# Fused memory attention and expert layer: the opening's loads, softmax and small tables in another order

## The chip, the cores and the metric

The kernel runs on one core of a Trainium2 chip. A core has five engines with queues of their own: TensorE (PE, and PEld for its weight loads), VectorE (DVE), ScalarE (ACT), GpSimd (POOL) and SyncE (SP, which issues most DMAs). The metric is device microseconds of one execution; lower is better.

## The reference

Eight batches, eight heads, 576 tokens, head size 64 and 32 memory slots. The attention output is the input of a gate that picks one of eight experts for each token.

```python
a = softmax(phi, axis=2)                    # phi: (8, 8, 576, 32), over the tokens
k_m = einsum('bhsm,bhsd->bhmd', a, k)       # 32 memory keys of each head
v_m = einsum('bhsm,bhsd->bhmd', a, v)
attn = softmax(q @ k_m.T / 8, axis=-1)      # (8, 8, 576, 32)
x = (attn @ v_m) as (4608, 512)             # heads side by side
logits = x @ w_gate + modality_bias[modality_id]
e = argmax(logits); gate_w = softmax(logits)[e]
out = gate_w * (relu(x @ w1[e]) @ w2[e])    # w1: (8, 512, 1024), w2: (8, 1024, 512)
```

## The kernel before

For each batch the kernel first builds the memory: the maximum of `phi` over the tokens (`first_max`, `mem_top`), exponentials (`mem_exp`), their sums (`mem_sums`), and products with `k` and `v` (`first_products`). The divided keys are turned by TensorE into `kT` and the values into `kvT` (`first_divide`, `first_odd`, `first_keys`, `first_values`). Scores (`first_scores`), a softmax over 32 slots (`soften`, `first_weights`) and a split in two parts of reduced precision (`first_split`: `xah` high, `xal` low) follow. The values are multiplied into the expert's first weights (`value_products`: `vwh` high, `vwl` low), so that the hidden layer (`hidden`, line 831) is a product of `xa` with `vw`, and the output (`outputs`, line 868) a product of `hh`/`hl` with `w2h`/`w2l`. `raw` is the expert's weights as loaded. All products of the expert stage are made three times (high by high, low by high, high by low).

The expert of the first token is guessed from the modality alone (`first_bias` on GpSimd, `preferred` and `guess` on VectorE), and its `w1` and `w2` are loaded by SP as soon as the guess is known. `mid` (the modality of all tokens) and `wg` (the gate's weights) are two small tables; `spread_row` spreads a row of the modality bias over all partitions by a product with ones, and ScalarE copies it to `known`.

Part 0 of batch 0 (256 of 576 tokens) is the opening. It is worked on in two groups of heads, `g` 0 and 1. The order of all instructions is made when the kernel is built: `plan_first` lists the steps of the opening in one order, `TAKES` gives each step's assumed time on each engine, and `weave` puts them between the experts' steps. Each engine then runs its own list strictly in that order. While TensorE would have nothing to do in the opening, `warm_small` and `warm` give it products of zeros that nobody reads, called fillers here (lines 168 and 161; `BUSY` says how many). TensorE's output banks are handed out from pools: `pair_of_banks(0)` is one buffer, so that a step that takes it waits until the reader of the step before is done.

## Time and profile before

| | |
|---|---|
| median of 3 runs | 379.02 us (378.89 to 379.66) |
| the profiled execution's own time | 379.99 us |
| its span, first to last instruction | 378.2 us |
| TensorE busy in the span | 370.8 us (98%) |
| VectorE, ScalarE, GpSimd busy | 248.5, 139.5, 45.9 us |
| granted clock of TensorE, mean | 0.995 |

The time is the span and 1.8 us around it. The granted clock has two levels in the profile's rows: 1.00 is 2.4 GHz, 0.50 is 1.2 GHz. Fillers count as busy, so the busy share does not tell how much of the opening is work.

### The profile page before, as it was taken

The page shows a single profiled execution, that of the slowest core. Times are in us where ns is not written, and L with a number is a line of the kernel's source. Part 1 is how long each engine was busy: PE and PEld are TensorE (multiplying, and loading weights), DVE is VectorE, ACT ScalarE, POOL GpSimd, SP SyncE. Part 2 cuts the span into 40 slices and gives each one's busy share as a digit, 9 for nine tenths or more (in the row PEclk, how much of TensorE's full clock was granted, in tenths as well). Part 3 has the DMA queues.
Part 4 walks back from the last instruction along what each step waited for, and adds up shares of the span by engine and source line. Part 5 has one row for each costly group of instructions (what it writes and reads, how often), then busy time and mean ns, then how long its engine had stood idle before and what let it go on. Part 6 is the DMA issues. An engine that isn't in the chain of part 4 may idle for free.

```text
span 378.2 us, 9988 instructions
## 1 busy us (share of the span) xinstructions
PE 370.8 (98%) x4045; PEld 309.8 (82%) x4045; DVE 248.5 (66%) x618; ACT 139.5 (37%) x328; POOL 45.9 (12%) x110
## 2 busy tenths in 40 slices
PE   7999999999999999999999999999999999999996
PEld 2767887889869897898987889797987979697986
DVE  4688767885958797868855689657874448750400
ACT  2283333534335055323414244431623306240401
POOL 3138030013130030004000030004000000000000
PEclk9899999999999999999999999999999999999999
DMA  8998769968958747583654637760232102321112
GB/s 289 348 378 233 111 98 279 285 116 269 316 107 257 259 73 137 170 301 61 111 166 131 239 69 133 204 212 2 56 99 86 29 2 55 119 63 30 31 34 56
DMA packets 93979, 56.89 MB, mean 150 GB/s; under 512 B 69732, under 2 KB 75108, under 8 KB 93924
## 3 DMA queue, kind: packets, MB, share of 16 engines
q1 hardware_dynamic: 93648, 55.87, 54.3%
q8 instruction: 33, 0.54, 0.6%
q10 hardware_dynamic: 276, 0.30, 0.2%
q14 instruction: 22, 0.18, 0.2%
HBM read 37.28 MB, written 18.87 MB: 148 GB/s over the span
## 4 chain that ended last, share of the span: by engine, by line
PE 92%; DVE 4%; DMA 1%; ACT 1%; issue 1%; ACTq 0%; POOL 0%; POOLq 0%; DVEq 0%
PE pe L868 49%; PE pe L831 27%; PE pair L408 4%; PE pe L776 2%; PE pair L571 2%; PE pe L912 2%; PE pair L713 1%; DMA row<-n_moe_modality_bias_dram 1%; PE pair L776 1%; PE pair L433 1%; PE pair L150 1%; PE pair L593 1%; PE pe L433 1%; DVE mx L628 0%; DVE a L624 0%
## 5 line engine op out<-in xcount | busy, mean ns | idle before, releaser
L868 PE MATMUL pe<-w2h,hh 128*128 128x512 f32 x280 | 111.2, 397 | 0.0
L868 PE MATMUL pe<-w2h,hl 128*128 128x512 f32 x280 | 109.3, 390 | 0.0
L868 PE MATMUL pe<-w2l,hh 128*128 128x512 f32 x280 | 107.1, 390 | 0.0
L848 DVE SCALAR_TENSOR_TENSOR hl<-pe,hh 128x256 fp32r<-128x256 f32 (+2 forms) x158 | 56.9, 390 | 37.5 <-ACT hh L844 36.7
L844 ACT ACTIVATE hh<-pe 128x256 fp32r<-128x256 f32 (+2 forms) x158 | 52.7, 362 | 32.9 <-PE pe L831 32.2
L868 PEld LDWEIGHTS pe<-w2h,hh 128*128 128x128 f32 x280 | 52.6, 188 | 12.0 <-DVE vwl L798 0.8
L868 PEld LDWEIGHTS pe<-w2l,hh 128*128 128x128 f32 x280 | 52.5, 188 | 11.2
L868 PEld LDWEIGHTS pe<-w2h,hl 128*128 128x128 f32 x280 | 52.6, 188 | 9.8
L881 ACT ACTIVATE ob<-pe,gates 128x512 f32<-128x512 f32 x35 | 23.9, 689 | 76.6 <-PE pe L868 38.9
L831 PE MATMUL pe<-xbh,vwh 128*128 128x320 f32 x128 | 40.2, 314 | 0.1
L831 PE MATMUL pe<-xbh,vwl 128*128 128x320 f32 x128 | 39.5, 309 | 0.0
L831 PE MATMUL pe<-xbl,vwh 128*128 128x320 f32 x128 | 39.5, 309 | 0.0
L831 PE MATMUL pe<-xah,vwh 128*128 128x256 f32 x124 | 35.2, 287 | 0.5 <-ACT xah L679 0.5
L831 PE MATMUL pe<-xah,vwl 128*128 128x256 f32 x124 | 34.9, 283 | 0.0
L831 PE MATMUL pe<-xal,vwh 128*128 128x256 f32 x124 | 34.9, 283 | 0.0
L831 PEld LDWEIGHTS pe<-xah,vwh 128*128 128x128 f32 x124 | 23.6, 191 | 2.8 <-ACT xah L679 1.6
L831 PEld LDWEIGHTS pe<-xbh,vwh 128*128 128x128 f32 x128 | 24.0, 188 | 1.4 <-issue 0.5
L344 POOL COPY ts<-tm 32x4 f32<-32x4 f32 x24 | 5.0, 210 | 164.4 <-DVE tm L336 163.6
L831 PEld LDWEIGHTS pe<-xbl,vwh 128*128 128x128 f32 x128 | 24.0, 188 | 0.3
L831 PEld LDWEIGHTS pe<-xbh,vwl 128*128 128x128 f32 x128 | 24.0, 188 | 0.0
L831 PEld LDWEIGHTS pe<-xal,vwh 128*128 128x128 f32 x124 | 23.7, 192 | 0.2
L831 PEld LDWEIGHTS pe<-xah,vwl 128*128 128x128 f32 x124 | 23.7, 192 | 0.0
(174 smaller groups left out, 466.7 us busy)
## 6 DMA issues: line engine op xcount, KB each, us to landing
out_dram<-ob SPq DMA_DIRECT2D x72, 128.0 KB, 2.4
q_sb<-in_q_dram SPq DMA_DIRECT2D x112, 72.0 KB, 3.1
kv_sb<-in_k_dram SPq DMA_DIRECT2D x6, 1152.0 KB, 6.3
kv_sb<-in_v_dram SPq DMA_DIRECT2D x6, 1152.0 KB, 9.7
ph<-in_phi_dram SPq DMA_DIRECT2D x13, 288.0 KB, 8.2
kv_sb<-in_k_dram SPq DMA_DIRECT2D x4, 576.0 KB, 6.0
kv_sb<-in_v_dram SPq DMA_DIRECT2D x4, 576.0 KB, 7.1
raw<-in_moe_w_dram SPq DMA_DIRECT2D x2, 1024.0 KB, 7.7
```

What stands on the lines that cost most here:

```text
L150: nc.tensor.transpose(dst, src, ident[:rows, :rows])
L344: nc.gpsimd.tensor_copy(ts_[BL * a:BL * (a + 1)], live["tm"][BL * o:BL * (o + 1)])
L408: nc.tensor.matmul(live["kvp"][M * j:M * (j + 1), g], lhsT=pe[half, j, c * M:(c + 1) * M], rhs=kv_sb[half, :, j, c * D:(c + 1) * D], start ...
L433: nc.tensor.matmul(to[g][M * j:M * (j + 2), 0:2 * D].rearrange("p (j d) -> p j d", j=2), lhsT=pe[half, c, j:j + 2].rearrange("p j m -> p ( ...
L571: nc.tensor.matmul(sc[g][M * j:M * (j + 1), a, 0:QC * BL], lhsT=kvT[b][rows, 0, M * j:M * (j + 1)], rhs=qT[rows, j, a], start=True, stop=T ...
L776: nc.tensor.matmul(pvs[g][M * j:M * (j + 1), :], lhsT=vT[b][rows, j, :], rhs=raw1[rows, j, cols], start=True, stop=not more, tile_position ...
L831: nc.tensor.matmul(ph[:, 0:n], lhsT=(vl if k == 2 else vh)[:, g, cols], rhs=xl if k == 1 else xh, start=(g == k == 0), stop=(g == NG - 1 a ...
L844: nc.scalar.activation(hs[0][:, f, h0:h0 + p1 - p0], live["ph", f][:, p0:p1], AF.Relu)
L848: nc.vector.scalar_tensor_tensor(hl, live["ph", f][:, p0:p1], 0.0, hh.bitcast(F32), op0=ALU.max, op1=ALU.subtract)
L868: nc.tensor.matmul(po, lhsT=tile_columns(hl if n == 1 else hh, f, t), rhs=(w2l if n == 2 else w2h)[:, f, :], start=(f == n == 0), stop=(f ...
L881: nc.scalar.activation(ob, po, AF.Copy, scale=gate_of(b, t))
L912: nc.tensor.matmul(po, lhsT=x, rhs=w2s[w][:, f, cols], start=(f == i == 0), stop=(f == FCH - 1 and i == 2),)
```

## The change

All of it is in the steps up to some 30 us. The halves of the first `phi` go out one behind the other on SP's queue, where one half went out on ScalarE's queue; the two tiny loads of ScalarE (`mid0` and the bias row) then come first there. `mid` and `wg`, which SP issued between the halves of `w1`, come behind the expert's weights and the rest of the queries. `preferred` stands ahead of the maximum's end. There is one small filler less ahead, and three more of 256 columns behind the exponentials' broadcast; `spread_row` moves from there behind the products with `v`. The first scores are made in two halves, each behind its own turn of the queries. In the softmax, group 1's subtraction and group 0's `xal` go to GpSimd. The first hidden products (`ha`) stand ahead of the value products of the second half of `w1`. `prepare` and `biases` (the modality tables, on GpSimd) come last.

```diff
-    BUSY = 64, 10
+    BUSY = 63, 10
...
         for hf in range(2):
             cols = slice(hf * 512, (hf + 1) * 512)
             nc.sync.dma_start(raw1[:, :, cols], first[:, :, cols])
-            if hf == 0:
-                load_rest()
...
         load_queries(0, RA, RB)
+        nc.sync.dma_start(wg, w_gate.rearrange("(a p) e -> p a e", p=P))
         load_phi(1)
+        load_rest()
...
             if step in (None, 2):
-                nc.vector.tensor_tensor(x, x, m.broadcast_to(list(x.shape)), op=ALU.subtract)
+                eng = nc.gpsimd if b == part == 0 and groups else nc.vector
+                eng.tensor_tensor(x, x, m.broadcast_to(list(x.shape)), op=ALU.subtract)
...
-            nc.vector.tensor_tensor(l, src, h.bitcast(F32), op=ALU.subtract)
+            (nc.vector if g else nc.gpsimd).tensor_tensor(l, src, h.bitcast(F32), op=ALU.subtract)
...
         add(("max", 0), "max0", [], first_max, floor=4.5)
+        add(("preferred",), "guess", [], preferred)
         add(("top", 0), "top0", [("max", 0)], mem_top, 0)
-        add(("preferred",), "guess", [], preferred)
         add(("guess",), "guess", [], guess)
         add(("exp", 0), "first exp", [("top", 0)], mem_exp, 0)
         nothing(2)
-        add(("known",), "nothing", [], spread_row)
+        nothing(3, 256)
...
         add(("v", 0), "v0", [("exp", 0)], first_products, 1)
+        add(("known",), "nothing", [], spread_row)
         add(("kT", 0), "kT", [("ko", 0)], first_keys)
         add(("vn", 0), "vn0", [("v", 0)], first_even, 1)
-        add(("s", 0, 0), "s0", [("kT", 0), ("qt", 0, 0, 1)], first_scores, 0, RA)
+        add(("s0", 0), "s0h", [("kT", 0), ("qt", 0, 0, 0)], first_scores, 0, RA, range(2))
+        add(("s", 0, 0), "s0h", [("s0", 0), ("qt", 0, 0, 1)], first_scores, 0, RA, range(2, HG))
...
-        add(("vw", 0, 1), "vwp", [], value_products, 0, 1, pair_(0))
-        add(("n", 0, 0, 1, 0), "n1", [("e", 0, 0, 1, 3)], first_weights, 1, 0)
-        some_hidden("ha", "h0c", [("xu", 0, 0, 0)], range(1), range(1))
+        add(("n", 0, 0, 1, 0), "n1", [("e", 0, 0, 1, 3)], first_weights, 1, 0)
+        add(("n", 0, 0, 1, 1), "n2", [], first_weights, 1, 1)
+        some_hidden("ha", "h0c", [("xu", 0, 0, 0)], range(1), range(1))
+        add(("vw", 0, 1), "vwp", [], value_products, 0, 1, pair_(0))
...
+        add(("prepare",), "nothing", [("w2", FCH - 1)], prepare)
+        add(("bias", 0), "nothing", [], biases, 0)
...
-        for half, eng in ((slice(HG // 2, HG), nc.scalar), (slice(0, HG // 2), nc.sync)):
-            eng.dma_start(phs[0][:, half], halves(phi, 0)[:, half])
+        for half in (slice(0, HG // 2), slice(HG // 2, HG)):
+            nc.sync.dma_start(phs[0][:, half], halves(phi, 0)[:, half])
```

TensorE's queue from the last of the ten big fillers to the products with `v`, before (`top` turned, `topc` broadcast, two fillers, the bias row, then `exp` with `k`, the `sums`, and `exp` with `v`, which goes to `pe`):

```order
L161 MATMUL pair_218<-busy 128x512
L150 MATMUL pair_264<-ident,top 128x128 [waits DVE_49,Pool_49]
L368 MATMUL pe<-ident,topc 64x128 [waits DVE_49]
L161 MATMUL pair_306<-busy 128x512 [waits PE_49]
L258 MATMUL pair_309<-row,ones_r 128x17 [waits DVE_49,DMAHW4_49,PE_49,Pool_49]
L433 MATMUL pair_318<-kv_sb,exp 64x128 [waits DMAHW3_49,Activation_49]
...
L444 MATMUL pair_318<-ones_c,sums 64x1 [waits DVE_49]
L433 MATMUL pe<-kv_sb,exp 64x128 [waits DMAHW5_49]
...
L150 MATMUL pair_414<-ident,keys 128x128 [waits DVE_49,Activation_49]
```

And of the change, at the same place:

```order
L161 MATMUL pair_217<-busy 128x512
L150 MATMUL pair_266<-ident,top 128x128 [waits DVE_49,Pool_49]
L367 MATMUL pe<-ident,topc 64x128 [waits DVE_49]
L161 MATMUL pair_305<-busy 128x512 [waits PE_49]
L161 MATMUL pair_308<-busy 128x256 [waits PE_49]
L432 MATMUL pair_318<-kv_sb,exp 64x128 [waits DMAHW4_49,Activation_49]
...
L443 MATMUL pair_318<-ones_c,sums 64x1 [waits DVE_49,Pool_49]
L432 MATMUL pe<-kv_sb,exp 64x128 [waits DMAHW5_49]
...
L257 MATMUL pair_414<-row,ones_r 128x17 [waits DMAHW2_49,PE_49,Pool_49]
L150 MATMUL pair_417<-ident,keys 128x128 [waits DVE_49,Activation_49]
```

The bias row's product went from ahead of the products with `k` to between those with `v` and the turn of the keys, which takes the same buffer `pair0` behind it; three fillers of 256 columns (one shown) stand where it stood.

TensorE's queue around the first hidden products, before (`kvT` with `raw` makes the value products; those that write a pair of banks behind line 790 are of the second half of `w1`):

```order
L776 MATMUL pe<-raw_104,kvT_78 32x512 x8
L790 MATMUL pe<-vwh,minus 128x512 [waits Activation_49] x2
L776 MATMUL pair_533<-raw_104,kvT_78 32x512 [waits DMAHW3_49,PE_49]
L776 MATMUL pair_533<-raw_104,kvT_78 32x512 x7
L831 MATMUL pe<-xah,vwh 128x256 [waits Activation_49]
L831 MATMUL pair_551<-xah,vwh 128x256 [waits DVE_49]
L831 MATMUL pe<-xal,vwh 128x256 [waits DVE_49]
L831 MATMUL pair_551<-xal,vwh 128x256 x2
```

Of the change:

```order
L776 MATMUL pe<-raw_104,kvT_78 32x512 x8
L790 MATMUL pe<-vwh,minus 128x512 [waits Activation_49] x2
L831 MATMUL pe<-xah,vwh 128x256 [waits Activation_49]
L831 MATMUL pair_534<-xah,vwh 128x256 [waits DVE_49]
L776 MATMUL pair_537<-raw_104,kvT_78 32x512 [waits DMAHW1_49,PE_49]
L776 MATMUL pair_537<-raw_104,kvT_78 32x512 x7
L831 MATMUL pe<-xal,vwh 128x256 [waits Pool_49]
L831 MATMUL pair_534<-xal,vwh 128x256 x2
```

The 16 value products moved behind the four products of `xah`, and the products of `xal` wait for GpSimd instead of VectorE.

VectorE's queue in the softmax of part 0, before (`a` the scores, `mx` their maxima, `sa` sums, `ra` their reciprocals, `aT` the turned weights; group 0 first, then group 1):

```order
L628 TENSOR_REDUCE mx_490<-a0_229 128x8
L666 TENSOR_REDUCE sa_497<-a0_229 128x8
L667 RECIPROCAL ra_498<-sa_497 128x8
L669 TENSOR_TENSOR a0_229<-a0_229,ra_498 128x8x32
L673 STREAM_TRANSPOSE aT_502<-a0_229 128x2x4x32
L630 TENSOR_TENSOR a0_229<-a0_229,mx_490 128x8x32
L681 TENSOR_TENSOR xal_110<-aT_502,xah_109 128x256
L666 TENSOR_REDUCE sa_542<-a0_229 128x8
```

Of the change:

```order
L627 TENSOR_REDUCE mx_481<-a0_228 128x8
L666 TENSOR_REDUCE sa_489<-a0_228 128x8
L667 RECIPROCAL ra_490<-sa_489 128x8
L669 TENSOR_TENSOR a0_228<-a0_228,ra_490 128x8x32
L673 STREAM_TRANSPOSE aT_494<-a0_228 128x2x4x32
L666 TENSOR_REDUCE sa_524<-a0_228 128x8
```

Two instructions (lines 630 and 681) left VectorE between the turn of group 0 and the sum of group 1.

## Rows read from the trace of the kernel before

**Rows 1.** Windows: stretch, length, busy (count) of PE, PEld, DVE, ACT, POOL, clock, DMA, GB/s

```profile
9.40:9.80 0.40, 0.40 (x16) 0.40 (x20) 0.29 (x1) 0.40 (x2) 0.00 (x0) 1.00 1.05 389
9.90:13.20 3.30, 3.30 (x76) 3.30 (x71) 1.62 (x4) 0.41 (x2) 0.00 (x0) 0.50 1.07 367
...
23.86:374.00 350.14, 349.95 (x3675) 296.98 (x3676) 233.60 (x578) 130.24 (x306) 39.52 (x69) 1.00 0.53 139
```

**Rows 2.** Timeline up to the exponentials: start, duration in us, what [idle before, releaser]

```profile
2.08 4.42 PE L161 MATMUL pair<-busy 128*128 128x512 bf16 x10
...
7.01 0.30 PE L150 MATMUL pair<-ident,top 128*128 128x128 f32 x1 [0.50 <-POOL mine L212]
...
4.68 2.18 DVE L310 TENSOR_REDUCE top<-ph 128x64 f32<-128x576 f32 x2 [4.68 <-DMA ph<-in_phi_dram]
...
8.23 1.46 DVE L375 TENSOR_TENSOR exp<-ph,pe 128x384 f32<-128x384 f32 x3
...
6.73 0.19 POOL L212 TENSOR_TENSOR mine<-row,is_n 1x8 f32<-1x8 f32 x1 [0.94 <-DMA row<-n_moe_modality_bias_dram]
...
1.25 0.45 SPq L184 DMA_DIRECT2D kv_sb<-in_k_dram  x1
1.75 0.52 SPq L184 DMA_DIRECT2D kv_sb<-in_v_dram  x1
```

**Rows 3.** DMA issues of the opening: size of one, us from issue to landing

```profile
kv_sb<-in_k_dram SPq DMA_DIRECT2D x1, 1152.0 KB, 7.4
...
kv_sb<-in_v_dram SPq DMA_DIRECT2D x1, 1152.0 KB, 9.9
```

**Rows 4.** Timeline from the bias row to the scores, by engine

```profile
8.77 0.36 PE L258 MATMUL pair<-row,ones_r 1*128 1x17 f32 x2
9.37 3.74 PE L433 MATMUL pair<-kv_sb,exp 64*64 64x128 f32 x72 [0.24 <-ACT exp L378]
...
13.04 2.26 PE L433 MATMUL pe<-kv_sb,exp 64*64 64x128 f32 x72
15.30 0.43 PE L150 MATMUL pair<-ident,keys 128*128 128x128 f32 x2
16.19 1.07 PE L593 MATMUL pair<-q_sb,kT 32*32 32x128 f32 x64 [0.46 <-ACT kT L534]
...
11.40 0.29 DVE L392 TENSOR_TENSOR sums<-sums,t2top 128x128 f32<-128x128 f32 x1
13.28 0.16 DVE L453 TENSOR_SCALAR den<-pair 128x2 f32<-128x2 f32 x1 [1.58 <-PE pair L444]
...
13.75 0.70 DVE L560 STREAM_TRANSPOSE q_sb<-q_sb 128x512 f32<-128x512 f32 x1
14.49 0.86 DVE L477 SCALAR_TENSOR_TENSOR keys<-pair,recs,even 128x64 f32<-128x64 f32 x4
...
10.15 0.16 ACT L259 COPY known<-pair 128x17 f32<-128x17 f32 x1
```

**Rows 5.** Timeline of the first hidden products and what they wait for

```profile
20.62 1.09 PE L776 MATMUL pair<-raw,kvT 64*32 64x512 f32 x16
21.64 0.51 PE L831 MATMUL pe<-xah,vwh 128*128 128x256 f32 x2
...
23.86 0.39 PE L831 MATMUL pe<-xah,vwh 128*128 128x256 f32 x1 [0.52 <-ACT xah L679]
...
19.02 0.42 DVE L628 TENSOR_REDUCE mx<-a 128x8 f32<-128x256 f32 x1
...
20.99 0.41 ACT L679 CAST xah<-aT 128x256 fp32r<-128x256 f32 x1 [0.84 <-DVE aT L673]
```

**Rows 6.** Timeline of GpSimd's subtractions, and of VectorE's use of the bias

```profile
32.29 2.55 POOL L924 TENSOR_TENSOR w2l<-ob,w2h 128x512 fp32r<-128x512 f32 x2
34.79 1.89 POOL L924 TENSOR_TENSOR w2l<-t2sums,w2h 128x512 fp32r<-128x512 f32 x1
...
41.44 0.19 DVE L728 TENSOR_TENSOR lg<-lgT,bias 128x32 f32<-128x32 f32 x1
```

More of the change, by code (lines that the diff above doesn't have):

```diff
@@ L156, in split, with warm @@
         nc.vector.tensor_tensor(l, src, h.bitcast(F32), op=ALU.subtract)
-    def warm(n, name="pa"):
-        idle = bank(name)
+    def warm(n, cols=512):
+        idle = bank("pa")
         for _ in range(n):
-            nc.tensor.matmul(idle, lhsT=busy[:, 0:P], rhs=busy, start=True, stop=True)
+            nc.tensor.matmul(idle[:, 0:cols], lhsT=busy[:, 0:P], rhs=busy[:, 0:cols], start=True, stop=True)
     def warm_small(n):
@@ L581, in scores, with first_scores @@
             load_queries(b + 2)
-    def first_scores(c0, n):
-        sc = [pair_of_banks(g) for g in range(NG)]
+    def first_scores(c0, n, js=range(HG)):
+        sc = [pair_of_banks(g) for g in range(NG)] if js[0] == 0 else live["sc", 0]
         qT = q_sb[0].rearrange("p j (c u t) -> p j c u t", u=2, t=BL)
@@ L588, in first_scores @@
         for u in range(2):
-            for j in range(HG):
+            for j in js:
                 for g in range(NG):
@@ L998, in add, with nothing @@
             stage(attention, name, kind, after, what, *args, floor=floor)
-        def nothing(n, name="pa"):
-            add(("nothing", len(attention)), "nothing", [], warm, n, name)
+        def nothing(n, cols=512):
+            add(("nothing", len(attention)), "nothing", [], warm, n, cols)
         def turns(part, k, floor):
@@ L1042, in plan_first @@
         add(("kvT", 0), "vT", [("vo", 0)], first_values)
-        add(("prepare",), "nothing", [], prepare)
-        add(("bias", 0), "nothing", [], biases, 0)
         for k in range(3):
```

14 lines of the change are left out of this document (6 added, 8 removed), and 2 rows, old and new, of the table TAKES.

## The prediction, made before the changed kernel ran

> **What bounds the kernel now.** I read the windows first, with the stretch in which TensorE never stops: from 23.86 to 374 it is busy for 349.95 of 350.14 us at the full clock [rows 1]. Nothing that the change moves behind 23.86 can shorten that; what the change is worth is how much earlier that stretch begins, that is, the first product of `xah` of group 1 at 23.86 [rows 5]. So I followed the chain of waits ahead of it. It goes: first half of `phi` landed and reduced from 4.68 to 6.86, maxima turned at 7.01, exponentials' subtraction at 8.23 [rows 2], products with `k` from 9.37, sums, divisor at 13.28, products with `v` from 13.04 to 15.30, turn of the keys at 15.30, scores at 16.19 [rows 4], then the softmax, group 0 and group 1. Second, the granted clock: 1.00 at 9.40 to 9.80, 0.50 (1.2 GHz) from 9.90 to 13.20 [rows 1]. Ahead of the fall TensorE had waited 0.50 us at the turn [rows 2] and 0.24 us at the products with `k` [rows 4], and in between ran the tiny product of the bias row. The 72 products with `k` took 3.74 us, and the 72 equal ones with `v`, from 13.04 and so nearly all behind that stretch, 2.26 us [rows 4].
>
> **The base of the sum.** The profiled execution took 379.99 us, 0.97 above the median of 379.02. Either that is a constant of profiling, or other executions meet the clock's fall elsewhere and lose less. The sum below is in the profiled execution's time; to state a median I take off half of 0.97, 0.49, and keep 0 and 0.97 as bounds. The Trainium skill (TensorE: Matmul & The Clock Gate, Part 1) says that the clock's monitor runs free of the kernel's start, so that one kernel meets cold stretches at different places. By that rule nothing is to be taken off, and the forecast below would read 379.25 instead of 378.8; no single profile can show it.
>
> **1. The logits' halves on one queue.** Two halves shared the DMA until shortly before 4.68. At the 389 GB/s of the window at 9.40 [rows 1] the 288 KB of one half take 0.76 us, so that a first half alone may be there at 3.92, and the two reductions of 2.18 us end at 6.10 instead of 6.86 [rows 2]. But the ten big fillers run from 2.08 to 6.50 [rows 2], and one small filler less does not change that: the turn goes at 6.54 instead of 7.01, **-0.47**. Bounds: 0 if the first half lands no earlier, -0.47 by the fillers. `preferred` now stands ahead of `topc` and needs `mine`, whose row of biases arrived at 6.73 [rows 2]; its DMA now goes out first on ScalarE's queue instead of behind half of `phi`. I take that it is in time; with the old latency and an issue 0.5 us earlier `topc` would be up to 0.36 late.
>
> **2. Up to the products with `k`.** What lies between turn and subtraction (1.22 us [rows 2]) is unchanged, so it starts at 7.76, and the products with `k` at 8.90 instead of 9.37. `k` landed at 1.25 + 7.4 = 8.65 [rows 2, 3], just in time. The three new fillers lie in TensorE's wait for the exponentials and cost nothing; if the clock were low there they would take some 0.64 us and still end about then.
>
> **3. The clock during `k`.** I take that it stays up: the tiny product is replaced by dense ones and the products with `k` begin earlier. Then 72 products at the rate of those with `v` take 2.26 us, to 11.16. The sums, at 11.69 before (11.40 + 0.29 [rows 4]), come 0.47 earlier, at 11.22, and are now what ends last. The divisor stood 0.2 us behind the last of the two: 11.45 instead of 13.28. If the clock falls at 9.85 as before, some 30 products are done by then; before, the 3.74 us were some 0.5 at 31 ns (15 products) and 3.25 for the other 57, 57 ns each, so that the last 42 end at 12.2.
>
> **4. `v` and the turn of the keys.** `v` landed at 1.75 + 9.9 = 11.65 [rows 2, 3]. Before that was hidden, now the products wait for it: 11.65 to 13.91, **-1.39** against 15.30. The keys take as long behind the divisor as before, 15.35 - 13.28 = 2.07 us [rows 4], so they are ready at 13.52 and do not decide. But the product of the bias row now stands between `v` and the turn, in the one buffer that the turn takes too: the turn waits for its 0.36 us and for ScalarE's copy of 0.16 [rows 4] with a handover of some 0.05 on either side, less 0.1 that overlaps the end of `v`. That is +0.55 (bounds 0.1 and 0.65): the turn starts at 14.46, **-0.84** in all. The turns of the queries (0.70 each [rows 4]) follow the keys, 13.55 to 14.95, and the scores start at 15.35 instead of 16.19; without the halves the second turn would still have been in time.
>
> **5. Softmax partly on GpSimd.** GpSimd's only large subtractions are of 512 elements, 2.55 us for two, 1.27 each [rows 6]. One of 256 costs between half, 0.64, and 1.27; I take 0.75. Relative to the scores' end two instructions of some 0.4 us each, like that of the maxima [rows 5], leave VectorE, and `xah` of group 1 is ready some 0.8 us earlier. **That is not where the gain is**, because TensorE's order changes too: before, the 16 value products (20.62 to 21.64) filled its wait for `xah` of group 0 (ready at 20.99 + 0.41 = 21.40), and all twelve hidden products followed, with 0.52 of idle to 23.86 [rows 5]: they end at 23.34, of which some 0.15 is the last one's tail, so that they hold TensorE for 1.55. Now four of them come first and wait until 21.44, then the value products (1.02 from start to start, by estimate 0.86 if their 1.09 ends in a tail), then the other eight: in the same frame 21.44 + 1.55 + 1.02 = 24.01, or 23.85 with the smaller figure. So 0 to +0.14, **+0.10**: the idle time has only moved ahead.
>
> **6. The small tables later.** `mid` and `wg` no longer break into the stream of the weights; the weights were not waited for, so 0. GpSimd's work on the tables comes behind its last subtraction, 34.79 + 1.89 = 36.68 [rows 6], and takes some 2.8 us; VectorE uses the bias at 41.44 [rows 6], so 2 us remain. If that cover went, gates and the first stores would come late and TensorE would wait for a bank.
>
> **Sum:** -0.84 + 0.10 = -0.74, 379.25 in the profiled execution's time, less 0.49: **378.8 us**, no change that can be measured (0.2%, 0.76 us, is about what a measurement of this kernel can tell from none).
>
> **Rivals.**
> *A, the forecast*: 378.28 (all 0.97 off) to 379.25 (none).
> *B, the clock falls all the same.* For it: the waits ahead of it are not gone, TensorE still waits for `topc` and the exponentials. Products with `v` then start at 12.3, 17 run at 57 ns until 13.25 and 55 at 31 ns, to 14.95; with the bias row the turn comes at 15.5, +0.2, and with +0.10 of step 5 it is +0.3: 379.3 to 380.3.
> *C, more than forecast*: `v` lands with the sums (-0.2) because nothing interleaves with SP's queue, the copy of the bias row is half hidden (-0.3), and the whole 0.97 is constant: 379.99 - 0.97 - 1.24 = 377.8. For it: at 389 GB/s the 2.9 MB of `phi`, `k` and `v` could have been in by some 10 us; against it, they landed at 11.65.
> *D, slower by GpSimd.* ScalarE takes its work in order, so the exponential of group 1, which waits for GpSimd's subtraction, stands ahead of `xah` of group 0. Group 1's maxima are ready at 19.44, `xah` could start at 20.99 [rows 5], and the exponential takes some 0.4 us like the cast: GpSimd may take 1.1 us before it shows; each further one puts the first hidden products, and all behind them, late by as much. The row at 34.79 shows 1.89 for one that ran beside VectorE, against 1.27 [rows 6]; at 1.89 it is +0.8, and with A's sum 379.1 to 380.05. Against it: that was twice as many elements. The Trainium skill (GPSIMD Engine Reference, Specifications) says that GpSimd shares its memory port with VectorE and collides with instructions of two inputs, and VectorE's scaling runs beside it here. By that rule it is nearer 0.95 than 0.64, still under the point; the 1.89 agrees with the rule.
> *E, the change does not do what it says*: one queue brings the halves no earlier, and the later issue of the second puts the maxima at the old time. Then `k` runs from 9.37 to 11.63 at the full clock, the sums come at 11.69, `v` from 11.92 to 14.18 with no wait for its landing, and the turn at 14.73: -0.57 + 0.10 = -0.47, 378.55 to 379.5.
>
> **How the numbers follow.** A 0.44, B 0.20, C 0.22, D 0.07, E 0.07. Faster by over 0.2% (under 378.26): all of C, a tenth of A at its lower end, and 0.07 of A for C's three terms when only one of them comes true, 0.33. Slower (over 379.78): 0.12 of B, whose middle is 379.8, and a third of D, 0.14. The rest, 0.53, is within 0.2%. The range goes from C's 377.8, cut to 377.9, to the middle of B's upper half and D, 379.6 to 379.8; 379.7.
>
> **What would show it.** The turn at 6.5 (step 1); products with `k` from 8.9 at a clock of 1.00 and ending at 11.2 (2, 3); products with `v` waiting for their DMA at 11.65 (4); the turn of the keys released by the copy of `known` (4); an idle TensorE of some 0.7 us ahead of the first hidden products, released by `xah`, and none ahead of those of group 1 (5); GpSimd's 256 elements at 0.64 to 0.95 (5, D); TensorE's stretch without a stop from about 23.1. I am wrong if the clock falls in another stretch, if `v` lands elsewhere, or if idle time turns up behind that stretch's start.

## The result and the profile after

The changed kernel takes 383.62 us (median, 383.32 to 384.66) against 379.34 of the kernel before on the same chip: ratio 1.0116, 95% interval 1.0096 to 1.0137. It is 1.2% slower, and the forecast of 378.8 (377.9 to 379.7) missed by 4.8 us. The profiled execution took 383.49 us with a span of 381.7; before it was 379.99 and 378.2, so all of the 3.50 us between these two lies inside the span. The medians differ by 4.28: the profiled execution of the kernel before was one of its slower ones (see the base of the sum, below).

TensorE's timeline of the changed kernel, from the turn of the logits to the first product of `xah` of group 1 (start, length, engine, line, operation, count, and in brackets the idle time ahead and what ended it), answers to [rows 2, 4, 5]:

```profile
6.07 0.30 PE L150 MATMUL pair<-ident,top 128*128 128x128 f32 x1
...
7.12 1.15 PE L161 MATMUL pair<-busy 128*128 128x512 bf16 x5
10.02 2.20 PE L432 MATMUL pair<-kv_sb,exp 64*64 64x128 f32 x72 [1.75 <-DMA kv_sb<-in_k_dram]
12.00 0.27 PE L443 MATMUL pair<-ones_c,sums 64*64 64x1 f32 x8
12.96 1.96 PE L432 MATMUL pe<-kv_sb,exp 64*64 64x128 f32 x59 [0.69 <-DMA kv_sb<-in_v_dram]
16.43 0.66 PE L432 MATMUL pe<-kv_sb,exp 64*64 64x128 f32 x13 [1.51 <-issue]
17.01 0.39 PE L257 MATMUL pair<-row,ones_r 1*128 1x17 f32 x2
17.67 0.44 PE L150 MATMUL pair<-ident,keys 128*128 128x128 f32 x2 [0.27 <-ACT known L258]
18.57 1.59 PE L592 MATMUL pair<-q_sb,kT 32*32 32x128 f32 x64 [0.46 <-ACT kT L533]
20.09 0.47 PE L150 MATMUL pe<-ident,values 128*128 128x128 f32 x1
20.92 1.73 PE L776 MATMUL pair<-raw,kvT 64*32 64x512 f32 x16 [0.35 <-ACT kvT L538]
...
23.44 0.97 PE L790 MATMUL pe<-vwh,minus 128*128 128x512 f32 x2
24.51 0.50 PE L831 MATMUL pe<-xah,vwh 128*128 128x256 f32 x2
...
27.26 0.40 PE L831 MATMUL pe<-xah,vwh 128*128 128x256 f32 x2
```

The reader is to see three things that [rows 4] don't have: waits for `k` and `v`; a stop of 1.51 us in the middle of 72 equal products, 59 ahead of it and 13 behind, which "issue" ends, that is, nothing that the profile shows; and, behind the stop, scores of 1.59 us instead of 1.07. The last comes from the clock. Windows of the changed kernel (length, TensorE busy, granted clock, DMA share, GB/s), and the last of them for the kernel before:

```profile
10.02:12.22 2.20, 2.20 (x80) 1.00 1.06 378
...
18.95:22.25 3.30, 2.94 (x73) 0.50 1.05 387
40.00:60.00 20.00, 19.57 (x289) 1.00 0.69 122
```

```profile
40.00:60.00 20.00, 19.85 (x324) 1.00 0.71 138
```

During `k` the clock now stays at 1.00 (before 0.50 [rows 1]); it falls behind the stop instead. And from 40 to 60 TensorE is busy for 0.28 us less than before. SP's own issues in the changed kernel:

```profile
0.74 0.97 SPq L1334 DMA_DIRECT2D ph<-in_phi_dram  x2
1.75 0.47 SPq L184 DMA_DIRECT2D kv_sb<-in_k_dram  x1
2.27 0.51 SPq L184 DMA_DIRECT2D kv_sb<-in_v_dram  x1
2.82 1.51 SPq L190 DMA_DIRECT2D q_sb<-in_q_dram  x2
7.97 1.25 SPq L230 DMA_DIRECT2D raw<-in_moe_w_dram  x2
```

And in the kernel before, where one half of `phi` went out here and the expert's first table stood later and in two pieces:

```profile
9.34 0.40 SPq L230 DMA_DIRECT2D raw<-in_moe_w_dram  x1
9.78 0.77 SPq L249 DMA_DIRECT2D mid<-in_moe_modality_id_dram  x1
10.60 0.61 SPq L253 DMA_DIRECT2D wg<-in_moe_w_gate_dram  x1
```

The landings in the changed kernel (KB, median us from issue), which answer to [rows 3]:

```profile
kv_sb<-in_k_dram SPq DMA_DIRECT2D x1, 1152.0 KB, 8.1
kv_sb<-in_v_dram SPq DMA_DIRECT2D x1, 1152.0 KB, 10.7
```

`k` is there at 1.75 + 8.1 = 9.85, `v` at 2.27 + 10.7 = 12.97: 1.2 and 1.3 us later than before. The chain point by point, in us of each trace:

| start of | before | forecast | after |
|---|---|---|---|
| turn of the logits | 7.01 | 6.54 | 6.07 |
| products with `k` | 9.37 | 8.90 | 10.02 |
| products with `v` | 13.04 | 11.65 | 12.96 |
| turn of the keys | 15.30 | 14.46 | 17.67 |
| scores | 16.19 | 15.35 | 18.57 |
| turn of the values | 17.19 | | 20.09 |
| `xah` of group 1 | 23.86 | 23.12 | 27.26 |

From first to last this is 27.26 - 23.86 = 3.40 us: -0.08 up to `v`; +1.79 in `v` (12.96 to 17.01 against 2.26), the stop and the restart; +0.66 for the bias row (17.01 to 17.67); +0.53 from the keys' turn to the values' (2.42 against 1.89) and +0.79 from there to line 790 (3.35 against 19.75 - 17.19), both at the low clock; -0.29 behind that. The other 0.10 of the 3.50 lies behind the table.

What the stop is can be read from the DMA's queues. Queue q8 carries instructions: 33 transfers of 16 KB in the whole span, for TensorE's 4047 products and as many weight loads, about 245 instructions each. The queues of the changed kernel over the whole span, and in the 0.02 us from 13.86:

```profile
q8 instruction: 33, 0.54, 0.6%
```

```profile
q8 instruction: 1, 0.02, 350.0%
```

This is the first q8 transfer of the span. It begins at 13.86, and TensorE goes on at 16.43, 2.57 us later. In the kernel before the first one begins at 11.36; 2.5 us behind that is 13.9, and TensorE, from 13.04 at the same pace, reaches its 59th product with `v` near 14.9: no stop.

### The profile page after: what moved, and what is told of

Read it like the earlier page. It is cut to its first block, busy times and chain, and to the rows that moved or that the text cites. A ratio compares the mean times of both kernels' runs of the same rounds, so it can differ in the third digit from the quotient of the medians.

```text
span 381.7 us, 9993 instructions
## 1 busy us (share of the span) xinstructions
PE 370.9 (97%) x4047; PEld 309.8 (81%) x4047; DVE 248.5 (65%) x616; ACT 139.3 (37%) x328; POOL 47.4 (12%) x112
## 4 chain that ended last, share of the span: by engine, by line
PE 94%; DMA 3%; ACT 1%; issue 1%; DVE 0%; SPq 0%; ACTq 0%; DVEq 0%
PE pe L868 51%; PE pe L831 27%; PE pair L407 4%; DMA kv_sb<-in_v_dram 3%; PE pe L776 2%; PE pair L570 2%; PE pair L776 2%; PE pe L912 2%; PE pair L713 1%; PE pair L150 1%; PE pair L592 1%; PE pe L432 1%; PE pair L831 0%; PE pair L545 0%; ACT vwh L785 0%
## 6 DMA issues: line engine op xcount, KB each, us to landing
kv_sb<-in_v_dram SPq DMA_DIRECT2D x6, 1152.0 KB, 10.7
```

## The experiments

The first question was what makes the stop. **Theory Q**: the single queue, with `phi`, `k`, `v` one behind the other, makes `k`, `v` and the instructions late. **Rival P**: TensorE's own new order. Ratios are to the kernel before, with the 95% interval.

**e1, the halves on two queues again** (changed kernel, one part undone):

```diff
-        for half in (slice(0, HG // 2), slice(HG // 2, HG)):
-            nc.sync.dma_start(phs[0][:, half], halves(phi, 0)[:, half])
+        for half, eng in ((slice(HG // 2, HG), nc.scalar), (slice(0, HG // 2), nc.sync)):
+            eng.dma_start(phs[0][:, half], halves(phi, 0)[:, half])
```

Expected: 

> The changed kernel with one part undone: phi's second half goes out on ScalarE's queue again. Theory Q (the single queue did it: k, v and TensorE's own block of instructions on queue q8 come late because everything stands in one queue): k lands near 8.7 and v near 11.7 us again, the q8 transfer starts by 11.5 instead of 13.86, the 1.51 us stop inside the products with v is gone, TensorE's clock stays up behind them, and the keys' turn comes at 14.5 to 15.5 instead of 17.67: 378.8 to 380.5 us. Rival P (the stop comes from TensorE's new order: more fillers, the bias row moved behind v): the stop of some 1.5 us stays, wherever k and v land, and the time stays at 382.5 or more.

Measured: 383.23 us, 1.0091 (1.0071 to 1.0112). Its timeline:

```profile
9.30 2.19 PE L432 MATMUL pair<-kv_sb,exp 64*64 64x128 f32 x72
...
11.88 1.94 PE L432 MATMUL pe<-kv_sb,exp 64*64 64x128 f32 x59
15.65 0.66 PE L432 MATMUL pe<-kv_sb,exp 64*64 64x128 f32 x13 [1.84 <-issue]
```

Half of Q holds: `k` and `v` are in time. Half of it falls: the stop stays, at the same product, and is longer, 1.84; q8 begins at 13.28. That, and the time, is what P had expected here.

**e2, the halves on one queue in the kernel before** (the same edit the other way). Expected: 

> The kernel before with this one part done: both halves of phi on SP's queue, first half first. Theory Q: k lands near 10.0, v near 12.9, the q8 transfer starts 2 us or more behind TensorE's 256th instruction, TensorE stops for 1 to 1.6 us inside or behind the products with v, and the time rises by 2 to 4 us, to 381 to 383.5. Rival P: no such stop, the turn of the logits comes at 6.1 to 6.5, and the time is 378.5 to 379.5.

Measured: 381.65 us, 1.0058 (1.0038 to 1.0077). `k` starts at 9.86 and takes 3.58 (clock at 0.50 from 10.48), `v` at 13.32, a stop of 0.85 behind 58 products, q8 at 13.83. So this one edit costs 2.4 us by itself (381.65 against 379.21), as Q said, and P, which had no stop here, does not hold alone. After e1 and e2 neither theory explains both runs.

**e3, TensorE's block of instructions at another place** (`BUSY = 63, 10` to `110, 9`). Expected: 

> The changed kernel with 110 small fillers at the start instead of 63, and 9 large ones instead of 10: the fillers end at the same time, but TensorE's 256th instruction stands 92 instructions earlier in its work, ahead of the products with k instead of in them. If the stop inside the products with v is TensorE waiting for its next block of instructions (queue q8), asked for at the 256th, then the q8 transfer starts 3 us earlier or so, the stop of 1.51 us is gone and the clock does not fall at 18.88: the scores end near 18.1 instead of 20.16, and the time falls to 380.5 to 381.5 us. k and v land as late as in the changed kernel. If the stop has another cause (a missing record of a wait, a full queue), it stays and the time is 383 to 384.

Measured: 386.5 us, 1.0193 (1.0174 to 1.0213), the slowest of all. The stop in `v` is gone and the clock no longer falls there; but the next block's end stands 92 instructions earlier too, and there a new stop appears:

```profile
13.23 2.20 PE L432 MATMUL pe<-kv_sb,exp 64*64 64x128 f32 x72 [0.68 <-DMA kv_sb<-in_v_dram]
...
16.91 1.14 PE L592 MATMUL pair<-q_sb,kT 32*32 32x128 f32 x63 [0.46 <-ACT kT L533]
19.39 0.26 PE L592 MATMUL pair<-q_sb,kT 32*32 32x128 f32 x1 [1.34 <-issue]
```

and more of the kind, 0.53 to 0.78 us each, far behind the opening (at 92.8, 152.2 and 204.0). TensorE has 47 small fillers more here and one large one less, and q8 has one transfer more:

```profile
q8 instruction: 34, 0.56, 0.6%
```

Both agree with q8 as the queue of TensorE's instructions: the stop moves with the block's end. The mechanism of the stop held, the forecast time did not: I had moved one block's end and forgotten those behind it.

**e4, the bias row ahead of `k` again** (`spread_row` behind the new fillers). Expected: 

> The changed kernel with the bias row's product back ahead of the products with k, behind the fillers. The prediction priced its place behind v at +0.55 on the way to the keys' turn. The trace of the changed kernel shows 17.09 for the end of the products with v and 17.67 for the turn, against 15.30 for both before: so 0.5 us less here if the stop in the products with v stays as it is, 382.6 to 383.3; if the tiny product ahead of k lets the clock fall during k, as it did before, those products take up to 1.5 us more, but v lands at 12.9 anyway: 0.2 us of loss at the most.

Measured: 382.65 us, 1.0091 (1.0060 to 1.0123), which overlaps the changed kernel's interval. In the trace TensorE restarts at 16.55 after a stop of 1.95 and turns the keys at 17.15, 0.60 later; in the changed kernel it is 1.24 (16.43 to 17.67). So in the traces the row's place costs 0.64; the times are too close to show it.

e1 left open what the instructions wait behind. The trace has each packet's start, length and size, not its DMA engine; strung together by end and start, packets of 2048 bytes, the size of the first expert's table, run directly ahead of each late q8 transfer, and packets of 1024, the queries', ahead of it in the kernel before. That is an order in time and proves no cause. **Theory W**: the table, asked for earlier, stands ahead of the instructions.

**e5, the table asked for later** (changed kernel):

```diff
-        add(("guess",), "guess", [], guess)
         add(("exp", 0), "first exp", [("top", 0)], mem_exp, 0)
+        add(("guess",), "guess", [], guess)
```

Expected: 

> The changed kernel with one edit: VectorE computes the number of the first expert behind the exponentials' subtraction and not ahead of it, so that SP issues that expert's tables some 2 us later (near 10.0 instead of 7.97). Runs so far: TensorE's transfer of instructions (q8) started at 13.86 in the changed kernel, 13.28 with phi on two queues again, 13.83 in the kernel before with phi on one queue, and each time packets of 2048 bytes, the first expert's table, ran ahead of it; in the kernel before it started at 11.36, ahead of those packets. Theory W (the transfer of instructions waits behind the expert's table, because the table is now asked for before it): q8 starts by 12.5, the stop of 1.51 us in the products with v is gone, the clock does not fall at 18.88, the turn of the keys comes near 15.9 instead of 17.67, and the time is 380.3 to 381.5 us. Theory Q (one queue full of phi, k, v is what it waits behind): q8 starts near 13.8 as before, the stop stays, 383 to 384 us. Both have k and v land at 10.0 and 12.9.

Measured: 381.9 us, 1.0065 (1.0035 to 1.0095), 1.7 us less than the changed kernel from two lines swapped. SP issues the table at 10.54; the stop shrinks by 0.99 to 0.52 (0.78 because q8 begins earlier, 0.25 because the products with `v` begin later), and the scores keep the clock:

```profile
15.69 0.66 PE L432 MATMUL pe<-kv_sb,exp 64*64 64x128 f32 x13 [0.52 <-issue]
...
17.83 1.15 PE L592 MATMUL pair<-q_sb,kT 32*32 32x128 f32 x64 [0.46 <-ACT kT L533]
```

W predicted no stop and q8 by 12.5; it came at 13.08. W and Q both have a part: with a table as late as this and `phi` on two queues (e9 to e11 and e14 below) q8 began by 11.5.

**e7, three fillers alone on the kernel before** (`nothing(3, 256)` ahead of the bias row). Expected: 

> The kernel before with one part of the change alone: three fillers of 256 columns ahead of the bias row and the products with k, for the clock. By the prediction's step 3 the clock then stays at 1.00 in the products with k (2.2 us instead of 3.74), the sums at 11.7 are what ends last, v has landed at 11.65, the turn of the keys comes at 14.1 to 14.4 instead of 15.30 and the time falls by 0.7 to 1.1 us, to 378.0 to 378.6. By theory W the expert's table and the transfer of instructions stand as close together as in the kernel before (9.34 and 11.36), so that there is no stop, unless the products with v reach the end of the loaded instructions before the block lands near 12.5 and is ready some 1.4 us later: then a stop of up to 0.6 us near 13.6 and 378.6 to 379.2. By the rival that the clock falls all the same the time is 379.0 to 379.5.

Measured: 379.32 us, 1.0008 (0.9987 to 1.0030). The clock stays up in `k` (2.19 us from 9.44), as step 3 had it, and `v` starts at 11.71 instead of 13.04. But q8 begins at 12.06, TensorE reaches the block's end sooner, and a stop of 1.00 takes the gain:

```profile
11.71 1.73 PE L433 MATMUL pe<-kv_sb,exp 64*64 64x128 f32 x55
14.45 0.70 PE L433 MATMUL pe<-kv_sb,exp 64*64 64x128 f32 x17 [1.00 <-issue]
15.08 0.44 PE L150 MATMUL pair<-ident,keys 128*128 128x128 f32 x2
```

So P has a part too: fillers alone, with two queues and the table at its old place, make a stop. And the table's issue is not all that sets the transfer: here it is at 9.17 and in e6 at 9.16, but q8 begins at 12.06 here and at 11.35 there. Why is not shown.

**e8, the small tables back** (changed kernel, step 6 undone). Expected: 

> The changed kernel with the small tables back in their old place (between the two halves of the first expert's first table) and GpSimd's work on them back behind the values' turn. SP's issue of the second half is then held back from near 8.6 to near 10, as the 0.77 and 0.61 us of issue for them did before. Theory W: the first half is still asked for at 7.97, some 2 us ahead of TensorE's instructions, so the stop stays, shorter only by what of the second half stood ahead of the transfer: 0.8 to 1.5 us, 382.5 to 383.5 us. If the small tables alone had kept the table away from the transfer, the stop is gone: 380.5 to 381.5. The prediction had this part at 0; the wait of 0.42 us at 46 that the changed kernel shows ahead of its first stores stays if it comes from TensorE being further ahead of VectorE there, and is gone if it comes from the bias table being late.

Measured: 383.38 us, 1.0090 (1.0058 to 1.0122); stop 1.60, q8 at 13.69: where the second half of the table stands matters little. The lost 0.28 us between 40 and 60 came back (19.85 busy), so that was step 6's; the time does not show it, because the clock was low until 24.55 in this profile.

**e6, step 5 alone on the kernel before** (softmax partly on GpSimd, `ha` ahead of the value products). Expected: 

> The kernel before with step 5 alone: group 1's subtraction and group 0's remainder on GpSimd, and the first hidden products ahead of the second half of the value products. The prediction had +0.10 for it (0 to +0.14), the idle time only moving ahead of the first hidden products: 379.2 to 379.5 us. Rival D (GpSimd late): up to +0.8. The trace of the changed kernel shows 0.62 and 0.74 us for GpSimd's two instructions, so D should not show; a gain of 0.3 to 0.5 would show that TensorE had waited for the softmax and not for itself.

Measured: 380.32 us, 1.0025 (1.0008 to 1.0041). Its timeline:

```profile
18.93 0.94 PE L791 MATMUL pe<-vwh,minus 128*128 128x512 f32 x2
21.25 0.50 PE L832 MATMUL pe<-xah,vwh 128*128 128x256 f32 x2 [1.38 <-ACT xah L680]
...
21.91 1.96 PE L777 MATMUL pair<-raw,kvT 64*32 64x512 f32 x16
```

The idle time did move ahead of the first hidden products, as step 5 said. It is 1.38 us, since `k` had the full clock here, and behind it the clock falls (0.50 from 21.89 to 25.31): value products of 1.96 instead of 1.09. **e12, the same with the value products first again**: expected: 

> The kernel before with GpSimd's part of the softmax alone: its two instructions there, and the second half of the value products ahead of the first hidden products, as in the kernel before. The run with step 5 whole took 380.32 us, and its trace shows TensorE waiting 1.38 us for xah of group 0 ahead of the first hidden products, and its clock falling at 21.89 behind that wait. Theory O (the order costs it): no such wait, no fall of the clock, 378.6 to 379.4 us. Theory G (GpSimd's instructions, or the waits between the engines, cost it): 380.0 or more.

Measured: 380.11 us, 1.0015 (1.0001 to 1.0028). The wait shrinks to 0.18 and the clock does not fall in this stretch, as theory O said, but this profile is not like e6's: its clock fell in `k` (3.86 us), as in the kernel before, and TensorE came later. The time is 0.21 less than e6's, within the noise, and lies in G's range, not in O's. What GpSimd's two instructions cost then is not shown.

Then kernels with several parts mended.

**e9** (e7 and the later table). Expected: 

> The kernel before with the three fillers ahead of k, as in the run with the fillers alone (turn of the keys at 15.08 with a stop of 1.00, 379.32 us), and with the number of the first expert computed behind the exponentials' subtraction, so that SP issues its tables near 10.4 instead of 9.17. Theory W: TensorE's transfer of instructions (q8), asked for near 9.6, starts at 11.2 to 11.6 instead of 12.06, the stop shrinks from 1.00 to 0.1 to 0.5, the keys turn at 14.3 to 14.7, and the time is 378.3 to 379.0 us. If the tables then land too late for the value products (an idle TensorE near 17 released by a DMA), 379.0 to 379.8. If the stop does not depend on when the table is asked for, it stays at 1.0: 379.1 to 379.5.

Measured: 380.37 us, 1.0017 (0.9998 to 1.0035). q8 at 11.24, no stop, keys' turn at 14.45. But the table is late: TensorE waits for `raw` 1.27 us at 17.94 and 0.60 at 21.35; and the bias row waits 0.77 for `star`, which the swap had also put later.

**e10** (changed kernel with e1, e4 and e5 together). Expected: 

> The changed kernel with three parts put right, each of which was run by itself: phi's second half on ScalarE's queue, the bias row ahead of k, the first expert's tables asked for behind the exponentials' subtraction. If the loss is made of the three that the traces show (k and v late by 1.3 us, the stop of 1.51 with the clock's fall behind it, the bias row's 0.58), k starts by 9.5, v by 11.9, q8 by 11.6, the stop is 0.5 at most, the keys turn at 14.3 to 14.8 and the time is 378.8 to 380.0; what is left above 378.5 would then be step 5's order, TensorE waiting for xah of group 0 ahead of the first hidden products (0.8 to 1.4 us). If 381 or more is left, something else costs time that no trace read so far shows.

Measured: 381.66 us, 1.0052 (1.0031 to 1.0072). No stop, q8 at 11.28, keys' turn at 14.57 as expected; the time was not, and the executions spread from 379.82 to 382.93. The profiled one is the fastest, so its trace does not show where the others lose. The four slowest had a mean granted clock of 0.990 or 0.991, the profiled one 0.999.

**e11** (e10 with the value products first). Expected: 

> As the run with three parts put right, and the second half of the value products ahead of the first hidden products again, as in the kernel before. Theory O (step 5's order, not GpSimd, is what is left): the wait for xah of group 0 is filled by value products, the stretch in which TensorE never stops begins 0.3 to 1.0 us earlier than with three parts, and the time is 378.0 to 379.0, 0.4 to 1.2 under that run. Prediction's step 5: the idle time only moves, within 0.15 of that run.

Measured: 381.16 us, 1.0036 (1.0021 to 1.0052): 0.50 under e10, as theory O said, though the intervals overlap, and 2 us above the time that O gave. Its profiled execution, the slowest of twelve, had the clock at 0.50 from 8.77 to 15.60 and `k` took 4.12 us, behind waits of 0.82, 0.72 and 0.46.

**e14** (e11, the bias row behind `k`). Expected: 

> As the run with three parts put right and the value products first, but the bias row's product behind the products with k instead of ahead of them: ahead of them it waited 0.77 us for the number of the first expert (DVE star), which the later request had put behind the exponentials' subtraction, and held up the products with k. Now k starts at 9.3 to 9.6 instead of 10.1 to 10.6, the row's product and ScalarE's copy lie in TensorE's wait for the sums or for v, q8 starts by 11.5 and the stop is 0.3 us at most. The keys turn at 14.2 to 14.6, TensorE's unbroken stretch begins at 22.8 to 23.3 instead of 23.86 of the kernel before: 378.0 to 379.2 us. If the clock falls in the waits ahead of k as in the run before it: 380 to 381.

Measured: 380.45 us, 1.0018 (1.0005 to 1.0032): three quarters of the loss are gone. `k` from 9.56, no stop; the clock fell in `k` (3.81 us), the keys turn at 16.01. That is the expectation's second case, but the fall is not what it misses the first by: the seven executions with a mean clock of 0.998 or more took 380.03 to 380.57.

**e13, `k` on ScalarE's queue** (changed kernel; `phi` stays on SP's):

```diff
-        load_kv(0, 0)
+        load_kv(0, 0, nc.scalar)
```

Expected: 

> The changed kernel with k alone sent out on ScalarE's queue instead of SP's; both halves of phi stay on SP's queue, first half first. In the six profiles with both halves on SP's queue the DMA moved 146 to 307 GB/s from 4 to 6 us, in the eight with the second half on ScalarE's 384 to 403, and k and v landed 1.3 us later in the former. Theory R (one queue alone cannot keep the engines full in this stretch, whatever stands in it): with k on a second queue the rate from 4 to 6 is 380 or more again, k lands by 8.9 and v by 11.9, and the turn of the logits still comes at 6.1 to 6.5. The stop inside the products with v stays (the first expert's tables are still asked for first): 382.0 to 383.4 us. Theory S (the slow stretch comes from phi's own packets, two halves of the same rows one behind the other in one queue): the rate from 4 to 6 stays under 330 and k lands near 9.5 or later.

Measured: 383.82 us, 1.0100 (1.0078 to 1.0123). Windows from 4 to 6 us (busy times of PE, PEld, DVE, ACT and POOL with their counts, clock, DMA share, GB/s), of the kernel before, the changed one, and e13:

```profile
4.00:6.00 2.00, 2.00 (x6) 0.59 (x4) 1.32 (x2) 0.00 (x0) 0.58 (x3) 1.00 1.03 390
```

```profile
4.00:6.00 2.00, 1.93 (x6) 0.54 (x4) 1.97 (x3) 0.00 (x0) 0.71 (x7) 1.00 0.89 295
```

```profile
4.00:6.00 2.00, 2.00 (x6) 0.59 (x4) 2.00 (x3) 0.00 (x0) 0.90 (x7) 1.00 1.06 407
```

Theory R holds in its rate: with a second queue in use the DMA moves 407 GB/s although `phi` is unchanged, and `v` lands 8.9 us after its issue at 1.75, near 10.65. `k`, now the one that shares, starts at 9.70, so its landing was missed by 0.8. Its clock fell (3.72 us for the 72 products), `v` began at 13.32 for that, and the stop is 0.75; the time is no better than the changed kernel's.

**e15** (e13 with e5's swap, the row behind `k` and the value products first). Expected: 

> The changed kernel with k on ScalarE's queue, the first expert's tables asked for behind the exponentials' subtraction, the bias row behind k and the value products ahead of the first hidden products: step 1's early turn (6.07) kept, and the three losses taken away. If theory R holds, k starts by 9.0, v by 11.9, the transfer of instructions starts ahead of the expert's tables, and the keys turn at 14.0 to 14.4: 377.8 to 378.8 us, faster than both. If theory S holds, k and v stay 1.3 us late, the keys turn at 15.2 to 15.6: 379.3 to 380.5.

Measured: 380.73 us, 1.0051 (1.0020 to 1.0082), in two heaps: seven executions at 379.9 to 380.74, five at 383.8 to 386.36; the mean granted clock was 0.998 to 1.000 in the lower heap and 0.985 to 0.996 in the upper one. The profiled one, 380.3, has the keys' turn at 14.64 and no stop in `v`, but a stop of 0.58 at the next block's end, in the value products.

**e16** (e14 without step 5) and **e17** (one large filler more). Expected: 

> As the run with the row behind k (380.45 us), with step 5 undone whole: group 1's subtraction and group 0's remainder on VectorE, value products and hidden products in the order of the kernel before. Step 5 by itself cost 0.94 us on the kernel before, and 0.73 with the order kept. If it costs as much here, 379.5 to 379.8 us, the same as the kernel before; if the stretch before it is now truly shorter (k from 9.5 at the full clock, no stop, v from 11.9), 378.4 to 379.2. If step 5 costs nothing here, 380.2 to 380.7, and what is left lies in the late small tables or in the clock's fall during k.

 And: 

> As the run without step 5, with eleven large fillers ahead of the logits' turn instead of ten, 0.2 to 0.4 us that lie in TensorE's wait of 0.86 for the maxima. If the waits of 0.4 to 0.9 us ahead of k decide whether the clock falls during k (3.81 instead of 2.2 us in the run with the row behind k), it falls less often: 0.2 to 0.6 us under the run without step 5. If not, within 0.2.

Measured: 380.45 us, 1.0030 (1.0021 to 1.0039), and 380.29, 1.0029 (1.0018 to 1.0041). Step 5 costs nothing on top of e14, against the 0.7 to 1.0 us that it cost on the kernel before, and one more filler is worth 0.16, within the noise, although the clock fell in none of e17's seven executions and in four of e16's eleven. e16's timeline:

```profile
12.04 2.46 PE L432 MATMUL pe<-kv_sb,exp 64*64 64x128 f32 x72
14.44 0.44 PE L150 MATMUL pair<-ident,keys 128*128 128x128 f32 x2
...
19.86 1.06 PE L775 MATMUL pair<-raw,kvT 64*32 64x512 f32 x9
21.21 1.06 PE L775 MATMUL pair<-raw,kvT 64*32 64x512 f32 x7 [0.30 <-issue]
```

The keys turn 0.86 us ahead of the profiled execution of the kernel before, and 0.12 of that is left at `xah` of group 1 (23.74): the 16 value products of the second half take 2.34 us from start to start (19.86 to 22.20) instead of 1.02 [rows 5], around the end of the next block of instructions; the kernel before had 0.52 us of idle time behind them, which is used up. From 40 to 60 it is busy for 19.58, step 6's loss again. No version beat the kernel before.

The runs together, by when SP issued the expert's first table, when the first q8 transfer began, and the stop in the products with `v` (e3, whose first transfer began at 4.82, is left out):

| run | table issued | q8 begins | stop |
|---|---|---|---|
| changed, e4 | 7.97, 7.96 | 13.86, 14.10 | 1.51, 1.95 |
| e13, e8 | 8.04, 8.31 | 13.57, 13.69 | 0.75, 1.60 |
| e2, e1 | 8.75, 8.88 | 13.83, 13.28 | 0.85, 1.84 |
| e7 | 9.17 | 12.06 | 1.00 |
| e6, e12, before | 9.16, 9.18, 9.34 | 11.35, 11.39, 11.36 | 0.23, 0, 0 |
| e5 (one queue) | 10.54 | 13.08 | 0.52 |
| e15, e9, e10 | 10.09, 10.73, 10.86 | 11.55, 11.24, 11.28 | 0, 0, 0 |
| e16, e11, e17, e14 | 11.05, 11.08, 11.14, 11.16 | 11.49, 11.41, 11.31, 11.41 | 0, 0, 0, 0 |

The executions apart by their mean granted clock, median time and number of each kind (the kernel before as it ran beside e16 and e17; in its profile one fall from 9.82 to 13.24 makes a mean of 0.995):

| kernel | 0.998 or more | lower |
|---|---|---|
| before | 378.88 (9) | 379.67 (8) |
| e7 | 379.12 (8) | 380.28 (2) |
| e9 | 379.56 (7) | 380.70 (5) |
| e14 | 380.24 (7) | 380.73 (5) |
| e16 | 380.28 (7) | 380.63 (4) |
| e17 | 380.29 (7) | none |

## Why the prediction was wrong

**The term that was missing** is the largest: TensorE's own instructions come by DMA, and the prediction has no step on them. Step 1 makes the guess of the expert ready sooner and step 6 takes the small tables out from between its pieces, so that SP asks for the table at 7.97 instead of 9.34. I counted that as free, since nobody waits for the table. The first block of instructions then came at 13.86 instead of 11.36, TensorE stopped for 1.51 us, and the clock fell behind the stop: 1.79 + 0.53 + 0.79 of the 3.40. e5 and the table above show the link to the table's issue, e8 that step 6 adds little to it (its stop is 1.60), e1 that it does not need the single queue, and e2 and e7 that one queue or the new fillers make a shorter stop with the table near its old time. That the table's packets hold the instructions up is the likely reason; no row shows the waiting itself.

**The base of the sum** was an execution of the wrong kind. The prediction left open what the 0.97 us between the profile and the median are. Of the 17 executions in the last table the eight at 0.995, the clock of the profiled one, took 379.51 to 379.75, and the nine at 0.998 or more 378.69 to 379.34: most of the 0.97 goes with a fall of the clock. Where it falls, an execution without a trace does not say. Of the 103 executions of the kernel before that ran beside the experiments, 64 had 0.998 or more. e6, whose work up to the keys' turn is that of the kernel before, shows an opening without it:

```profile
9.19 2.20 PE L433 MATMUL pair<-kv_sb,exp 64*64 64x128 f32 x72 [0.23 <-ACT exp L378]
...
14.47 0.44 PE L150 MATMUL pair<-ident,keys 128*128 128x128 f32 x2
```

The forecast for the changed kernel was 14.46. So most of the -0.84 of steps 1 to 4 was won against the fall in one profile and not against the usual execution, and taking off a part of the 0.97 as well counted the same gain twice. By this, the median would have been about that of the kernel before even without the stop.

**Steps 2 and 4, the landings.** "`k` landed at 1.25 + 7.4 = 8.65" took SP's issue time of the kernel before. The change itself puts the second half of `phi` ahead of `k`, so the issue is at 1.75: 0.5 us that could have been read off the diff and the 0.46 of one issue. The other 0.7 to 0.8 is rate: 295 instead of 390 GB/s from 4 to 6, and 346 instead of 397 from 6 to 8.4, which is 0.19 and 0.12 MB, 0.8 us at 390. e1, e2 and e13 show that it goes with the number of queues in use. Why one queue is slower here is not shown.

**Step 1** was right and undersized: the maxima began at 3.72 (forecast 3.92), the ten fillers ended at 5.93 (3.86 us instead of 4.42), because the clock, by the trace's record of it, rose at 5.22 instead of 6.41, and the turn came at 6.07 instead of 6.54. Rival E falls. The gain was lost whole in the wait for `k`.

**Step 3** was right in this execution: the clock stayed up in `k`, and 72 products took 2.20 us against 2.26 forecast. Of the fifteen profiles with the five fillers it stayed up in twelve, of the four without in one (e6). Rival B is therefore not excluded for an execution, and e6 and the kernel before, whose work up to `k` is the same, differ in it. The Trainium skill (TensorE: Matmul & The Clock Gate, Part 1) says that the clock's monitor runs free of the kernel's start; by that rule such differences are expected, and these two traces agree.

**Step 4, the bias row**: +0.55 forecast, 0.64 in the traces of e4 and the changed kernel. Right.

**Step 5**: GpSimd's two instructions were priced rightly (0.64 to 0.95; they took 0.62 and 0.74), and rival D's lateness did not come:

```profile
22.42 0.62 POOL L630 TENSOR_TENSOR a<-a,mx 128x256 f32<-128x256 f32 x1 [17.63 <-DVE mx L627]
24.54 0.74 POOL L681 TENSOR_TENSOR xal<-aT,xah 128x256 fp32r<-128x256 f32 x1 [1.50 <-ACT xah L679]
```

The +0.10 was too small: alone on the kernel before step 5 cost 1.0 (e6, 380.32 against 379.34), and 0.7 with the old order (e12). In e6's profile the clock answered to the moved wait, but its three executions at 1.000 took 379.84, 380.46 and 381.38, so the fall is not shown to be the price. In the changed kernel its stretch shows as -0.29, probably because the softmax caught up during the slow value products.

**Step 6**: not 0; its 0.28 us between 40 and 60 come back when it is undone (e8). TensorE waits for a bank there, as the prediction's warning had it:

```profile
47.43 0.41 PE L831 MATMUL pe<-xbh,vwh 128*128 128x320 f32 x1 [0.42 <-ACT ob L881]
```

The same wait of 0.42 stands in e14 and e16, which keep step 6, and not in the kernel before or e8. But the cover that the warning named did not go: GpSimd's work on the bias ended at 43.04 and VectorE used it at 45.00. What makes `ob` late is open.

**What stays open.** e14 and e16 take away every loss found in the opening and still take 1.0 and 1.1 us more than the kernel before. e16's profiled execution (380.25) is only 0.26 above the profiled one of before (379.99), but the two are of different kinds: its clock did not fall, the other's did. Like with like it is 1.4 us (380.28 against 378.88). Some 0.2 to 0.3 of that is step 6; the value products around the second block's end took 1.3 us longer than in the profile of before (2.34 against 1.02), and if the 0.52 us of idle time behind them there takes up its part, 0.8 is left. That is an estimate, and the rest is open: no trace of the kernel before without the fall is on record.

## What to carry to other kernels

A step that nobody waits for is not free if it issues DMAs: ask what else has to come by DMA then, TensorE's instructions included, and where in the work the ends of its 16 KB blocks fall. When a load is moved ahead of another in one queue, add its issue time to every landing behind it before using a latency of the old trace. Before a profile becomes the base of a sum, compare its mean granted clock with those of the other executions: a gain against a fall of the clock that most executions do not have is no gain in the median.

## What the runs showed of the hardware

**TensorE stops for its instructions.** In the nine kernels of the table with a stop, TensorE went on 2.37 to 2.61 us after the q8 transfer began (16.43 - 13.86 in the changed kernel, 15.65 - 13.28 in e1), and the transfer itself took 1.1 us. The Trainium skill (Runtime: NRT & Kernel Launch, Instruction fetch mechanics) says that the sequencer fetches blocks of 16 KiB, 256 instructions, over a DMA queue of its own and that the cost is mostly hidden; the 33 transfers agree with the block, the stops of up to 1.95 us do not agree with "mostly hidden" in a stretch where the DMA is full (a share of 1.06 from 10.02 to 12.22). When a transfer was asked for stands in no row, so how long it waited is not shown.

**One queue moved less than two.** From 4 to 6 us the DMA moved 146 to 307 GB/s in the six profiles with `phi`, `k` and `v` all in SP's queue, and 384 to 410 in those with one of them on ScalarE's.

**Behind a stop the clock can fall.** The stops of 1.51, 1.60, 1.84 and 1.95 us in the products with `v` were each followed by a granted clock of 0.50, from 18.88, 17.72, 17.21 and 18.11 on; the five shorter ones there, up to 1.00, were not, nor was e3's 1.34 us in the scores.
